# Spare products for PE in the idle gaps of a transformer block's head, and evacuations chosen by what is ready

## Chip, cores, metric

One core of a Trainium2 chip. The metric is device microseconds of one execution, median over the timed executions. PE is TensorE, ACT ScalarE, DVE VectorE, POOL GpSimd, SP the engine that issues most transfers.

## The reference

A pre-norm transformer block on 2048 tokens of width 1024: multi-query attention (32 query heads of 32, one key and value head), then a gated feed-forward part of width 3584, both with a residual. Cut to what matters:

```python
h  = x + A(layernorm(x), wq, wk, wv, wo)          # softmax((x@wq) @ (x@wk).T * Dh**-0.5) @ (x@wv) @ wo
h2 = h + B(layernorm(h), w_gate, w_up, w_down)    # (sigmoid(g) * u) @ w_down
```

## The kernel before

The kernel is written by a scheduler of its own: a Python plan with an estimated duration for each instruction decides, at build time, the order on every engine, and the program is then emitted in that order with semaphores. So an edit to the plan can move instructions far from the edited line.

The head of the program normalizes the 16 tiles of x on DVE, turns tiles 0 to 3 by transposes on PE and the others by DMA, and makes K, V and the first Q. The kernel lays out eight banks in PSUM for what PE writes: two (`F_ps`) for Q, K, V, transposes and everything else, six (`S_ps`) in three pairs for scores. What leaves a bank is copied by ACT or DVE; `evac` chooses by the work already queued on each:

```python
def evac(fn_act, fn_dve, n, deps, prio, dve_rate=0.96):
    now = pl.free["pe"]
    a = max(pl.free["act"], now) + sum(o.occ for o in pl.heap["act"]) + n / 1.2
    d = max(pl.free["dve"], now) + sum(o.occ for o in pl.heap["dve"]) + n / dve_rate
    ...                                   # the smaller sum takes the copy (after the first scores with an offset for ACT)
# transposes of x tile t, half hf, leave their bank always by ACT:
e = pl.op("act", fa, [last], prio=1, **t_act(512))
```

When the plan finds nothing for PE, it issues a product whose result nobody reads, if an F_ps bank is free, else it lets PE wait:

```python
if v == 0 and known([c_w], t):            # v: score blocks issued so far; warm-up products
    pl.op("pe", mm(S_ps[:, 5, 0:P], hact[:, 0:P], hact[:, 0:P], True, True), [c_w], ...)
...
spare = [b for b in range(2) if known(bank_rel[b], t) and ...]
if v and spare:
    ...                                   # a product into the free F_ps bank
pl.free["pe"] = t + 20.0                  # otherwise PE waits
```

The softmax here doesn't subtract the row's maximum and nothing guards it: scores larger than these inputs give would overflow.

## Time and profile before

| | before |
|---|---|
| median of 3 runs | 1081.42 us (1079.97 to 1081.45) |
| span of the profiled run | 1079.0 us |
| PE busy | 1069.8 us, idle 9.2 us |
| clock of PE over the span | 0.998 of full |
| half clock | 19.358 to 22.771 us |

The prediction below shows the page, windows of 5 us and timelines. One more view is of use for what comes: the same windows laid so that they begin and end where the half clock does. The columns are start:end, length, busy time of PE, PE's weight loads, DVE, ACT and POOL (in brackets the instructions), the granted clock, the DMA share and GB/s.

```profile
15.94:19.36 3.42, 1.57 (x19) 1.06 (x20) 3.32 (x8) 3.42 (x7) 0.00 (x0) 1.00 0.87 306
19.36:22.77 3.41, 3.41 (x30) 2.20 (x28) 2.90 (x9) 0.67 (x3) 0.94 (x2) 0.50 0.02 5
```

In the first stretch PE works less than half of the time (1.57 of 3.42 us) at full clock; in the next its clock is 0.50 throughout.

The changes of the clock lie whole steps of 3.4133 us apart (3.413 in what follows). In this trace's clock record it is full from 5.705 us for 13.653 us (4 steps), half for 3.413 us (1 step), and full again for 1058.132 us (310 steps). I call a step a window, and the one just before a half clock the window that decided. That it decides is my reading, not something that a trace records.

### The profile page before, as it was taken

The numbers are of one execution on the slowest core, as the hardware profiler recorded it, in microseconds if no ns is written. First come the engines' busy times: TensorE is split into PE (matmuls) and PEld (weight loads), VectorE is DVE, ScalarE is ACT, GpSimd is POOL, SyncE is SP. The second block draws the span as 40 slices with busy tenths as digits, with TensorE's granted clock in tenths as the row PEclk, the third lists the DMA queues.
The fourth block names the chain that finished last, engine by engine and source line by source line (L and its number), as shares of the span: only waits on it lengthen the run. The fifth ranks groups of instructions, "written<-read, shape, count | busy, mean of one in ns | idle before, by whom it ended". The sixth has DMA issues, their size and how long they took to land.

```text
span 1079.0 us, 31597 instructions
## 1 busy us (share of the span) xinstructions
PE 1069.8 (99%) x13080; PEld 490.4 (45%) x13080; DVE 902.3 (84%) x1735; ACT 1009.7 (94%) x1168; POOL 30.7 (3%) x58
## 2 busy tenths in 40 slices
PE   8999999999999999999999999999999999999999
PEld 7764444444444444444444444444444444444445
DVE  7889998898989879898888989898887988888721
ACT  6999999999999999999999999999999999999700
POOL 2100000000000000000000000000000000000000
PEclk9999999999999999999999999999999999999999
DMA  8898898939679795969879594965969489887994
GB/s 227 166 282 267 210 286 229 269 92 285 169 210 220 154 278 123 271 141 253 198 177 272 133 277 105 277 168 155 264 168 275 108 232 201 217 224 162 287 275 113
DMA packets 308623, 227.14 MB, mean 211 GB/s; under 512 B 119808, under 2 KB 299904, under 8 KB 308480
## 3 DMA queue, kind: packets, MB, share of 16 engines
q1 hardware_dynamic: 307296, 224.92, 82.2%
q8 instruction: 103, 1.69, 0.7%
q14 instruction: 40, 0.33, 0.2%
q10 hardware_dynamic: 1184, 0.20, 0.1%
HBM read 195.17 MB, written 7.86 MB: 188 GB/s over the span
## 4 chain that ended last, share of the span: by engine, by line
PE 88%; ACT 10%; issue 1%; DMA 1%; DVE 1%; SPq 0%
PE F_ps L414 69%; PE S_ps L414 18%; ACT Pr L706 9%; ACT tnh L1008 1%; DMA ring<-in_B_w_up_dram 0%; DMA ring<-in_A_x_dram 0%; DVE Rc L805 0%; ACT zone L289 0%; DVE Ts L740 0%; DVE st L345 0%; ACT QTb L289 0%; PE F_ps L443 0%; DVE st L347 0%; DVE ring L383 0%; PE S_ps L443 0%
## 5 line engine op out<-in xcount | busy, mean ns | idle before, releaser
L706 ACT ACTIVATE Pr<-S_ps 128x1024 bf16<-128x1024 f32 x1024 | 970.1, 1168 | 4.1 <-PE S_ps L414 3.5
L740 DVE TENSOR_TENSOR Ts<-Ts,Pr 128x1024 bf16<-128x1024 bf16 x736 | 481.0, 676 | 33.9 <-ACT Pr L706 31.7
L414 PE MATMUL F_ps<-ring,hnT 128*128 128x512 bf16 (+1 forms) x1957 | 417.0, 380 | 1.7 <-issue 0.7
L414 PEld LDWEIGHTS F_ps<-ring,hnT 128*128 128x128 bf16 (+1 forms) x1957 | 147.7, 97 | 187.8 <-issue 48.5
L414 PE MATMUL F_ps<-zone,hact 128*128 128x512 bf16 (+2 forms) x1164 | 209.4, 377 | 0.7 <-issue 0.7
L414 PE MATMUL S_ps<-QTb,kT 32*128 32x256 bf16 x4096 | 207.2, 273 | 0.1
L414 PEld LDWEIGHTS S_ps<-QTb,kT 32*128 32x128 bf16 x4096 | 63.6, 92 | 206.8 <-ACT Pr L706 152.9
L414 PE MATMUL F_ps<-Pr,Vb 128*32 128x256 bf16 x4064 | 134.2, 274 | 0.0
L414 PEld LDWEIGHTS F_ps<-zone,hact 128*128 128x128 bf16 (+1 forms) x1164 | 75.0, 97 | 83.5 <-issue 23.0
L414 PEld LDWEIGHTS F_ps<-Pr,Vb 128*32 128x32 bf16 x4064 | 96.8, 96 | 29.9 <-issue 16.7
L740 DVE TENSOR_TENSOR Ts<-Pr 128x1024 bf16<-128x1024 bf16 x128 | 86.5, 683 | 25.7 <-ACT Pr L706 25.3
L1012 DVE SCALAR_TENSOR_TENSOR hst<-tnh,F_ps 128x512 bf16<-128x512 f32 x107 | 73.2, 684 | 38.4 <-PE F_ps L414 36.8
L1008 ACT ACTIVATE tnh<-F_ps 128x512 f32<-128x512 f32 x105 | 78.5, 747 | 5.7 <-PE F_ps L414 5.7
L414 PE MATMUL F_ps<-zone 128*128 128x256 bf16 (+4 forms) x667 | 75.7, 276 | 0.5 <-ACT QTb L289 0.4
L414 PE MATMUL F_ps<-wo_sb,OT 128*128 128x512 bf16 (+1 forms) x294 | 60.9, 380 | 0.2 <-issue 0.2
L414 PEld LDWEIGHTS F_ps<-zone 128*128 128x128 bf16 (+1 forms) x667 | 44.0, 98 | 23.1 <-issue 7.4
L747 DVE TENSOR_TENSOR Ts<-Ts 128x1024 bf16<-128x1024 bf16 x64 | 43.9, 686 | 1.1
L357 POOL TENSOR_SCALAR zb<-mvb 128x1 bf16<-128x1 bf16 (+1 forms) x25 | 9.9, 396 | 994.5 <-DVE mvb L349 994.5
L1008 ACT ACTIVATE tnh<-S_ps 128x512 f32<-128x512 f32 x7 | 4.2, 597 | 35.3 <-PE S_ps L414 35.3
L290 DVE COPY Oc<-F_ps 128x256 f32<-128x256 f32 x60 | 25.3, 421 | 11.5 <-PE F_ps L414 10.7
L414 PEld LDWEIGHTS F_ps<-wo_sb,OT 128*128 128x128 bf16 (+1 forms) x294 | 20.9, 97 | 26.7 <-issue 7.4
L795 DVE TENSOR_TENSOR Oc<-F_ps,Oc 128x256 f32<-128x256 f32 x59 | 24.9, 422 | 7.4 <-PE F_ps L414 6.2
(81 smaller groups left out, 414.2 us busy)
## 6 DMA issues: line engine op xcount, KB each, us to landing
ring<-in_B_w_gate_dram SPq DMA_DIRECT2D x318, 256.0 KB, 4.7
ring<-in_B_w_up_dram SPq DMA_DIRECT2D x316, 256.0 KB, 4.6
zone<-in_B_w_down_dram SPq DMA_DIRECT2D x28, 256.0 KB, 3.6
h_sb<-in_A_x_dram SPq DMA_DIRECT2D x16, 256.0 KB, 4.5
out_dram<-h_sb SPq DMA_DIRECT2D x31, 128.0 KB, 3.1
ring<-in_A_x_dram SPq DMA_DIRECT2D x7, 512.0 KB, 5.1
QTb<-q_scratch SPq DMA_DIRECT2D x14, 256.0 KB, 5.4
Pr<-in_B_w_gate_dram SPq DMA_DIRECT2D x10, 256.0 KB, 4.2
```

Of the source, the lines that this page charges most:

```text
L290: lambda: DVE.tensor_copy(out=out_ap, in_=in_ap))
L357: f = pl.op("pool", lambda: POOL.tensor_scalar(out=zb[:, ph, sl].unsqueeze(2), in0=mvb[:, ph, sl, 1:2], scalar1=LN_EPS_BF16, scalar2=None, ...
L414: fn = lambda: PE.matmul(o, lhsT=l, rhs=r, start=start, stop=stop, **kw)
L706: exps[u] = pl.op("act", lambda slot=slot, pb=pb: ACT.activation(out=pslot(slot).rearrange("p (a b) -> p a b", a=2), in_=S_ps[:, pb:pb + 2 ...
L740: o = pl.op("dve", lambda T=T, a=a, b=b: DVE.tensor_tensor(out=T, in0=a, in1=b, op=ALU.add), deps, prio=4, **t_dve(1024, 1.92))
L747: merge_ev[G] = pl.op("dve", lambda T4=T4: DVE.tensor_tensor(out=T4[:, :, 0, :], in0=T4[:, :, 0, :], in1=T4[:, :, 1, :], op=ALU.add), [sum ...
L795: a = pl.op("dve", lambda: DVE.tensor_tensor(out=Oc[:, :], in0=O, in1=Ob, op=ALU.add), [last, oc_ev[G], o_ev.get(G - 1)], prio=0, **t_dve( ...
L1008: tanh_of[n] = pl.op("act", lambda: ACT.activation(out=tnh[:, :], in_=FB(b), func=ACTF.Tanh, scale=0.5), [last, tn_user.get(0)] + (tn_more ...
L1012: e = pl.op("dve", lambda: DVE.scalar_tensor_tensor(out=hst[:, n % NST, :], in0=tnh[:, :], scalar=1.0, in1=FB(b), op0=ALU.add, op1=ALU.mul ...
```

## The change

Its intent: PE should not go idle in the head, so that the work there (and the clock) goes on; ACT, which is full there, should give copies to DVE while DVE waits for x. The diff in full:

```diff
 def evac(fn_act, fn_dve, n, deps, prio, dve_rate=0.96):
     now = pl.free["pe"]
-    a = max(pl.free["act"], now) + sum(o.occ for o in pl.heap["act"]) + n / 1.2
-    d = max(pl.free["dve"], now) + sum(o.occ for o in pl.heap["dve"]) + n / dve_rate
+    ready = now + 300.0 if v < 2 else 1e9
+    a = max(pl.free["act"], now) + sum(o.occ for o in pl.heap["act"] if o.ready <= ready) + n / 1.2
+    d = max(pl.free["dve"], now) + sum(o.occ for o in pl.heap["dve"] if o.ready <= ready) + n / dve_rate
@@ transposes of x @@
-    e = pl.op("act", fa, [last], prio=1, **t_act(512))
+    e = evac(fa, fd, 512, [last], 1) if t > 1 else pl.op("act", fa, [last], prio=1, **t_act(512))
@@ nothing found for PE @@
+    if 0 < v < 16 and not spare and known([exps[2 * v - 1]], t):
+        k = 2 * ((2 * v - 1) % NB)
+        enter("full")
+        pl.op("pe", mm(S_ps[:, k, 0:P], ident[:, :], ident[:, :], True, True), [c_id, exps[2 * v - 1]], **t_mm(P)).tag = "dummy"
+        continue
```

## The prediction

> **What bounds the kernel now.** I read the page first (busy shares, the clock row, the chain of work that ended last), then windows of the head, then the timelines of PE, ACT and DVE there.
>
> ```profile
> PE 1069.8 (99%) x13080; PEld 490.4 (45%) x13080; DVE 902.3 (84%) x1735; ACT 1009.7 (94%) x1168; POOL 30.7 (3%) x58
> PE 88%; ACT 10%; issue 1%; DMA 1%; DVE 1%; SPq 0%
> ```
>
> PE is idle for 1079.0 - 1069.8 = 9.2 us of the whole span, and PE and ACT together are 98% of the chain. So nothing that fills idle time can be worth 2% (21.6 us); what can be won is a few microseconds, and they lie in the head. Windows of 5 us show where:
>
> ```profile
> core 0: us, PE busy (x) PEld busy (x) DVE busy (x) ACT busy (x) POOL busy (x), PEclk, DMA share, GB/s
> 10.00:15.00 5.00, 5.00 (x99) 4.19 (x97) 4.00 (x11) 3.76 (x9) 1.12 (x2) 1.00 1.08 361
> 15.00:20.00 5.00, 3.01 (x38) 2.15 (x35) 3.96 (x10) 4.52 (x9) 0.55 (x2) 0.94 0.74 247
> 20.00:25.00 5.00, 5.00 (x72) 3.47 (x70) 3.21 (x10) 2.74 (x6) 0.40 (x1) 0.72 0.38 75
> 25.00:30.00 5.00, 4.55 (x61) 3.21 (x59) 4.41 (x13) 5.00 (x9) 0.92 (x2) 1.00 0.81 167
> ```
>
> PE loses 2 us at 15 to 20 us; then the granted clock falls to 0.72 on average while ACT is nearly half idle. Quarter-microsecond windows put the half clock (0.50) from about 19.36 to 22.77 us, 3.41 us long. The timeline of PE shows what came before it (start, length, what):
>
> ```profile
> 15.40 0.40 PE L443 MATMUL F_ps<-ident,ring 128*128 128x128 bf16 x4
> 16.59 0.89 PE L443 MATMUL F_ps<-ident,ring 128*128 128x128 bf16 x8 [0.80 <-ACT QTb L289]
> 18.49 0.40 PE L443 MATMUL F_ps<-ident,ring 128*128 128x128 bf16 x4 [1.01 <-ACT zone L289]
> 18.98 3.07 PE L414 MATMUL F_ps<-zone 128*128 128x128 bf16 x23
> 21.98 0.61 PE L414 MATMUL S_ps<-QTb,kT 32*128 32x256 bf16 x8
> ```
>
> From 15.40 to 18.98 PE does nothing but 16 transposes of x tiles 2 and 3, and it waits for ACT to empty the two F_ps banks. What ACT does then:
>
> ```profile
> 14.95 0.39 ACT L289 ACTIVATE QTb<-F_ps 128x256 bf16<-128x256 f32 x1
> 15.21 1.04 ACT L706 ACTIVATE Pr<-S_ps 128x1024 bf16<-128x1024 f32 x1
> 16.12 0.42 ACT L289 ACTIVATE QTb<-F_ps 128x256 bf16<-128x256 f32 x1
> 16.38 0.65 ACT L289 ACTIVATE zone<-F_ps 128x512 bf16<-128x512 bf16 x1
> 16.86 1.08 ACT L706 ACTIVATE Pr<-S_ps 128x1024 bf16<-128x1024 f32 x1
> 17.76 1.76 ACT L289 ACTIVATE zone<-F_ps 128x512 bf16<-128x512 bf16 x3
> 22.64 1.02 ACT L706 ACTIVATE Pr<-S_ps 128x1024 bf16<-128x1024 f32 x1 [1.67 <-PE S_ps L414]
> ```
>
> ACT works without a gap from 13.13 to 19.5 us, so here ACT sets PE's pace; then it starves until the slow PE delivers the next scores at 22.64. DVE meanwhile stands:
>
> ```profile
> 13.47 0.88 DVE L394 TENSOR_SCALAR ring<-ring,rstd 128x1024 bf16<-128x1024 bf16 x2
> 16.04 0.69 DVE L345 BATCH_NORM_STATS2 st<-ring 128x6 f32<-128x512 bf16 x1 [1.69 <-DMA ring<-in_A_x_dram]
> 24.05 0.23 DVE L290 CAST Vb<-F_ps 128x64 bf16<-128x64 f32 x1 [1.79 <-ACT kT L289]
> ```
>
> [...] half clock lasted 3413 ns, and the last clock change before it, at 5.705 us, lies four such windows ahead (5.705 + 4 x 3.413 = 19.357). So the window that decided was 15.944 to 19.357. [...] that window held 12 transposes (12 x 0.056 = 0.67 us at their spacing) and 7 matmuls (0.39 us), together 31%, and lost the clock; the next emptiest at full clock were at 67% or more and kept it. [...]
>
> **The change, part by part.** The three edits look as if the scheduler might reshuffle everything, so I compared the order of instructions on each engine. It hardly moves: SP and POOL are identical, and after the first half dozen score blocks nothing differs anywhere.
>
> *Evacuations.* Two QTb copies go from ACT to DVE and one Vb copy from DVE to ACT. The new choice for x tiles 2 and 3 changes nothing: their four zone copies stay on ACT. The first QTb copy (12.33) lay before the wait for the first scores (13.13) and is worth nothing. The second (14.95) lies in the gapless ACT stretch: 15.21 - 14.95 = 0.26 us earlier for all that follows, so the next F_ps copies, PE's transposes and the Q products at 18.98 come at about 18.7. On DVE the first delays the norm of tiles 2 and 3: a copy of 0.4 us, less the 0.21 us that DVE waits there for POOL anyway, some 0.2 to 0.3 us; they are ready near 14.6 and are used at 15.2 or later. The second falls into the 1.69 us in which DVE waits for x. Both are free. The Vb copy costs ACT about 0.10 us: a QTb copy of 0.38 us takes 0.26 us of ACT's time, and a Vb copy lasts 0.16 us less (0.22).
>
> *Products.* Fourteen products with the identity are added: nine after the third set of transposes, five after the fourth. At 0.056 us apart that is 0.50 and 0.28 us. The nine wait for the exponential at 16.86 (done near 17.6 after the shift); then PE would have waited till about 18.1 for its bank anyway. The five end near 18.7, where Q can start. They cost at most 0.05 us.
>
> *Clock.* The window 15.944 to 19.357 would now hold 12 transposes (0.67), 14 products (0.78) and Q products from 18.7 on (0.66): 2.1 us or 62%, against 31%. If that keeps full clock, these go away: nine 128-column matmuls at 0.107 instead of 0.056 us, 0.46; seven 256-column ones at 0.213 instead of 0.109, 0.73; from the first score matmul to its exponential 0.66 instead of 0.45 (as at 12.68 to 13.13), 0.21; the change to score mode 0.04. Sum 1.44 us.
>
> *Does it reach the end?* ACT is gapless again from 22.64 to 27.25, then PE runs from 27.30 with almost no wait, the same order as before. If all engines come earlier by the same amount, the end does too. Not everything moves: the transposes by DMA of tiles 4 and 5 still go out at 21.77, the second near 23.1; with 3.6 us to landing they are there near 27. They are first used near 30.4 us by my count of matmuls, 28.8 after the shift, so 1.8 us of slack. The later tiles hang on DVE, which no longer stands 1.79 us before a Vb copy, so they come earlier as well.
>
> Sum: 0.26 + 1.44 - 0.10 - 0.05 = 1.55 us at 27 us, carried whole to the end. 1081.4 - 1.55 is 1079.9; I say **1079.8 us**.
>
> **The rivals.**
> *A, the clock still falls.* The products are few, and [...] no window at full clock between 31% and 67% tells me where the limit is. Then 0.1 to 0.2 us are left: 1081.2. I give it one in four.
> *B, the half clock was not in every run before.* [...] the three timed runs were 1081.45, 1081.42 and 1079.97: the odd one is 1.46 us faster, just my 1.44. If before often escaped, after gains only 0.1 us on those runs, but its own time is the same 1079.8. What speaks against an escape as the rule: two timed runs and the profiled one (1081.3) are slow. B alters the difference, not the prediction.
> *C, a wait takes the place.* PE comes 1.6 us early and meets data not yet there: the transposes by DMA, the weights, or ACT, which is 94% busy. For it: DVE is full from 30 to 45 us. Against it: the weight loads are released by exponentials, which move too, and the order is the same. It would give back part: 1080.5 to 1081.
> *D, more comes out.* DVE freed by 1.8 us could take away small waits for its copies at 28 to 50 us; PE's idle time there is only some tenths: 1079.3.
>
> **Range and chances.** Main case two in three at 1079.8 with about 0.7 us to either side for run to run spread; A and C pull up to 1081.3. So 1078.7 to 1081.4 eight times in ten. Faster by over 2% or slower by over 2% would take 21.6 us, more than twice all of PE's idle time, and nothing late in the order changed: 0.005 each, 0.99 within 2%.
>
> **What would show it.** Right: the clock at 1.00 through 15 to 25 us; the 23 matmuls after the last transposes in about 1.65 us instead of 3.07; the third pair of exponentials starting near 21.0 instead of 22.64; no DVE wait for kT near 22 us; the span shorter by about 1.5 us. The evacuations alone are seen in Q starting near 18.7. Wrong if the half clock is still there or moved to another window (A), if PE shows new waits after 28 us for DMA or ACT (C), or if the products delay the fourth set of transposes beyond 18.2.

Passages are cut where marked: what was said there about the cause of the half clock, about transposes and about the order in which ACT and DVE work, none of which a trace of this case had shown when it was written. That the full clock, and with it the 1.44 us, would follow from a fuller window was at that time my estimate, from one trace with one window at 31% that lost the clock and none at full clock below 67%.

## The result

| | before | after |
|---|---|---|
| first round, 4 runs each | 1081.41 us (1079.97 to 1081.45) | 1080.24 us (1079.78 to 1080.59) |
| profiled span | 1079.0 us | 1078.0 us |
| clock over the span | 0.998 | 1.000 in all four runs |

The ratio is 0.9992, with a 95% interval of 0.9975 to 1.001: the same within 2%. Ratios are the mean time of one kernel's fast runs over that of the other's of the same rounds, so not quite the ratio of the medians quoted here.

The page of the changed kernel:

```profile
PE 1043.5 (97%) x12925; PEld 489.3 (45%) x13094; DVE 903.2 (84%) x1736; ACT 1009.8 (94%) x1167; POOL 30.6 (3%) x58
PE 73%; ACT 19%; issue 4%; DVE 2%; DMA 1%; SPq 0%; DVEq 0%
```

PE's 97% is no loss: 13094 weight loads stand beside 12925 matmuls, so 169 records of matmuls are missing in this trace. Where they are missing PE seems to wait for "issue" (from 100 to 1000 us 19.5 us in 112 waits, against 1.6 us in 6 in the kernel before). I therefore compare starts, not PE's busy time.

The same windows of 5 us as in the prediction:

```profile
15.00:20.00 5.00, 3.70 (x59) 3.17 (x57) 3.54 (x8) 4.41 (x9) 0.21 (x1) 1.00 0.76 263
20.00:25.00 5.00, 4.24 (x82) 3.28 (x83) 5.00 (x15) 4.28 (x8) 1.63 (x4) 1.00 0.29 55
```

The clock is 1.00 in both; from 20 to 25 us ACT is busy for 4.28 instead of 2.74 us, because scores reach it earlier. The timeline of PE in that stretch:

```profile
15.39 0.39 PE L444 MATMUL F_ps<-ident,ring 128*128 128x128 bf16 x4
16.46 0.89 PE L444 MATMUL F_ps<-ident,ring 128*128 128x128 bf16 x8 [0.69 <-ACT QTb L290]
17.87 0.68 PE L415 MATMUL S_ps<-ident 128*128 128x128 bf16 x9 [0.52 <-ACT Pr L707]
18.38 0.39 PE L444 MATMUL F_ps<-ident,ring 128*128 128x128 bf16 x4
18.61 0.44 PE L415 MATMUL S_ps<-ident 128*128 128x128 bf16 x5
18.89 1.82 PE L415 MATMUL F_ps<-zone 128*128 128x128 bf16 x23
20.64 0.40 PE L415 MATMUL S_ps<-QTb,kT 32*128 32x256 bf16 x8
```

The 9 and 5 products fill the wait before and after the fourth set of transposes, and the 23 matmuls take 1.82 instead of 3.07 us. ACT and DVE:

```profile
16.00 0.40 ACT L290 ACTIVATE QTb<-F_ps 128x256 bf16<-128x256 f32 x1
17.65 1.75 ACT L290 ACTIVATE zone<-F_ps 128x512 bf16<-128x512 bf16 x3
21.09 1.02 ACT L707 ACTIVATE Pr<-S_ps 128x1024 bf16<-128x1024 f32 x1 [0.72 <-PE S_ps L415]
```

```profile
14.48 0.42 DVE L291 CAST QTb<-F_ps 128x256 bf16<-128x256 f32 x1
16.45 0.69 DVE L346 BATCH_NORM_STATS2 st<-ring 128x6 f32<-128x512 bf16 x1 [1.55 <-DMA ring<-in_A_x_dram]
```

The exponential that began at 22.64 now begins at 21.09; the second moved copy lies on DVE in its wait for x.

Since the order is the same, each of the 1024 exponentials can be set beside its twin. I call the difference of their starts the **lead**. It is -0.15 us at the first pair (this execution's x simply came 0.15 us later), 1.55 us at the third, 1.45 from the moved Vb copy on, and 1.44 us as far as 125 us. Then something takes a part back: at 141 us it is 1.01, from 185 us to the end 0.97 us. The timeline of PE names it:

```profile
139.15 0.59 PE L415 MATMUL F_ps<-ring,hnT 128*128 128x512 bf16 x2 [0.43 <-DMA ring<-in_B_w_up_dram]
151.79 0.61 PE L415 MATMUL F_ps<-ring,hnT 128*128 128x512 bf16 x2 [0.86 <-DMA ring<-in_B_w_up_dram]
```

PE waits twice for weights that it did not wait for before. So three questions were open: does the clock make the gain, and which part of the change keeps it; does the kernel before always lose the clock; and are the late weights the price of the lead or chance?

### The profile page after: what moved, and what is told of

It reads as the page before. It is cut to its first block, busy times and chain, and to the rows that moved or that the text cites. A ratio compares the mean times of both kernels' runs of the same rounds, so it can differ in the third digit from the quotient of the medians.

```text
span 1078.0 us, 31453 instructions
## 1 busy us (share of the span) xinstructions
PE 1043.5 (97%) x12925; PEld 489.3 (45%) x13094; DVE 903.2 (84%) x1736; ACT 1009.8 (94%) x1167; POOL 30.6 (3%) x58
## 4 chain that ended last, share of the span: by engine, by line
PE 73%; ACT 19%; issue 4%; DVE 2%; DMA 1%; SPq 0%; DVEq 0%
PE F_ps L415 57%; ACT Pr L707 18%; PE S_ps L415 16%; ACT tnh L1009 1%; DVE Ts L741 1%; DMA ring<-in_B_w_up_dram 1%; DVE Rc L806 0%; DMA ring<-in_A_x_dram 0%; DVE st L346 0%; DVE Oc L796 0%; DVE hact L291 0%; DVE st L348 0%; PE F_ps L444 0%; DVE Oc L291 0%; DVE Ts L748 0%
## 5 line engine op out<-in xcount | busy, mean ns | idle before, releaser
L415 PE MATMUL F_ps<-ring,hnT 128*128 128x512 bf16 (+1 forms) x1870 | 400.7, 380 | 13.1 <-issue 8.5
L415 PE MATMUL F_ps<-zone,hact 128*128 128x512 bf16 (+2 forms) x1106 | 197.5, 377 | 9.5 <-issue 9.0
L415 PE MATMUL F_ps<-zone 128*128 128x256 bf16 (+4 forms) x658 | 72.2, 272 | 2.3 <-issue 1.1
L415 PE MATMUL F_ps<-wo_sb,OT 128*128 128x512 bf16 (+1 forms) x283 | 58.4, 380 | 1.7 <-issue 1.6
```

The source lines that it names most:

```text
L415: fn = lambda: PE.matmul(o, lhsT=l, rhs=r, start=start, stop=stop, **kw)
```

## The experiments

Each kernel ran five times, with nine runs of the kernel before on the same chip in between (three such groups of four kernels). For every execution the granted clock is recorded: 1.000, or 0.998 where it had one window of half clock (3.413 us at 0.50 in a span of 1079.0 us, in the first trace). I write "kept" and "lost" for these. All results were correct. Groups of five are small, so single counts (three lost, two kept) are weak; what the account rests on is all runs together.

### Evacuations alone, products alone, thin products, and the change again

The first experiment leaves out the products. The order on all engines is then that of the changed kernel, less 14 matmuls.

```diff
-            if 0 < v < 16 and not spare and known([exps[2 * v - 1]], t):
-                ...                      # the products
```

> The evacuation part alone: the order of instructions is that of the changed kernel less its 14 products. Theory (the clock makes the gain): PE loses the clock for one window of 3.41 us in the head again[...]; such runs take 1081.2 to 1081.6 us, and the profile's third pair of exponentials starts near 22.4 us. Rival (the evacuations make the gain, the products only fill idle time): 1080.3 us, no half clock needed for it.

Measured: 1081.1 us median; three runs lost the clock (1081.7, 1081.1, 1081.4), two kept it (1079.74, 1079.77). In the trace, which lost it, the lead is 0.27 us after the fourth exponential (0.32 less the 0.05 that it already had at the first); the third pair begins at 22.34.

```profile
18.16 0.40 PE L444 MATMUL F_ps<-ident,ring 128*128 128x128 bf16 x4 [1.01 <-ACT zone L290]
18.65 3.10 PE L415 MATMUL F_ps<-zone 128*128 128x128 bf16 x23
```

The 23 matmuls take 3.10 us at half clock, as before. The evacuations give their 0.27 us and do not keep the clock.

The second adds only the products, and leaves every copy where it was; PE's order differs from before in these 14 alone.

```diff
+            if 0 < v < 16 and not spare and known([exps[2 * v - 1]], t):
+                ...                      # the products; evac() and mk_xT() as before
```

> The 14 products alone, every evacuation where the kernel before had it: the order differs from before in these 14 matmuls only. Theory: full clock through the head in every run (granted clock 1.000), third pair of exponentials near 21.3 us instead of 22.64, some 1080.2 us. Rival (evacuations make the gain): 1081.4 us as before, with or without the half clock.

Measured: 1081.36 us; three lost (1081.59, 1082.62, 1081.36), two kept (1080.15, 1079.77). Here my theory, as I had put it, fell: the products alone do not keep the clock either.

```profile
18.12 0.74 PE L414 MATMUL S_ps<-ident 128*128 128x128 bf16 x9 [0.52 <-ACT Pr L706]
18.66 0.63 PE L443 MATMUL F_ps<-ident,ring 128*128 128x128 bf16 x4
19.62 2.98 PE L414 MATMUL F_ps<-zone 128*128 128x128 bf16 x23
```

The nine products are there, from 18.12 on, and the fourth set of transposes runs at half clock, which begins at 18.60. The window that decided, 15.185 to 18.598, ended as the ninth product started: it held nearly all of the nine, but neither the fourth set nor the five products after it.

The third is the changed kernel unedited, for a second trace.

> The changed kernel once more, unedited, for a second trace and five more rounds beside the others on one chip. If the 0.5 us given back between 125 and 165 us comes from a stretch in which the weight transfers fill the DMA engines, PE waits for weights there again (two waits of about 0.4 and 0.9 us in the first trace) and the lead falls from 1.44 to about 1.0 us. If that was chance in one run, the lead stays 1.44 to the end and the time is 1079.8 us.

Measured: 1079.82 us (1079.74 to 1079.96), all five kept. The lead is 1.60 us at 27 us and still 1.57 at 900 us, and PE has no wait for weights. So the late weights of the first trace are not the regular price of the lead.

The fourth lets each product stream 16 columns instead of 128.

```diff
-mm(S_ps[:, k, 0:P], ident[:, :], ident[:, :], True, True)
+mm(S_ps[:, k, 0:16], ident[:, :], ident[:, 0:16], True, True)
```

> The changed kernel with each of its 14 products streaming 16 columns instead of 128: same count, same places, same waits, but about an eighth of the streaming (14 x 0.025 us at the spacing of small matmuls). Theory (what counts is how much PE streams in a window): the half clock comes back in runs whose window falls on the transposes, 1081.2 to 1081.6 us. Rival (the presence of products, or their waits, makes the gain; streaming doesn't matter): 1080.3 us at full clock.

Measured: 1081.28 us; four lost (1080.95, 1081.28, 1081.51, 1081.42), one kept (1079.70). Count, places and waits are those of the changed kernel, so here it is the streaming of the products that counts, not that they are there. (The 0.025 us of the expectation can be seen in the first trace of before: 32-column matmuls start so far apart from 22.78 us on. On this chip 10 of these 15 runs of incomplete kernels lost the clock, 4 of the 9 of before, and none of the 5 of the changed kernel.)

### The kernel before again, and transposes in place of the products

> The kernel before, unedited, for a second trace and more runs. Theory [...]: about half of the runs lose the clock (granted clock 0.998) and take 1.0 to 1.5 us longer than those that keep it; if the traced run kept it, its windows, counted from its first full clock, all hold over 42% of streaming; if it lost it, the lost one holds under 37%. Rival (the loss belongs to the kernel, not to the phase): all runs lose it, at 1081.4 us.

(The cut parenthesis is the theory that a run loses the clock when a window happens to fall on the stretch of transposes; in the first six traces the windows there began anywhere from 14.19 to 15.94 us.) Measured: 1080.0 us, **all five kept** (1079.83 to 1080.37); the nine interleaved runs of the same kernel on the same chip kept it six times and lost it three times (1081.42, 1081.8, 1081.43). Here is the timeline of the same program as before, in an execution that kept its clock:

```profile
18.98 1.83 PE L414 MATMUL F_ps<-zone 128*128 128x128 bf16 x23
20.75 0.40 PE L414 MATMUL S_ps<-QTb,kT 32*128 32x256 bf16 x8
```

Up to 18.98 it is the execution of the prediction to the hundredth; then 1.83 instead of 3.07 us. Its lead over the first trace is 1.44 us from the third pair to the end, which is the price of one lost window measured by itself. The rival "the loss belongs to the kernel" falls. Where it kept the clock, windows of 3.413 us counted from its first full clock (4.146 us) hold 80, 37.5 and 63% of streaming; I had expected over 42% for the emptiest.

Next, the 14 products become 14 transposes of the identity:

```diff
-mm(S_ps[:, k, 0:P], ident[:, :], ident[:, :], True, True)
+lambda k=k: PE.transpose(out=S_ps[:, k, :].bitcast(BF16)[:, 0:P], in_=ident[:, :], identity=ident[:, :])
```

> The changed kernel with its 14 products turned into 14 PE transposes of the identity into the same idle score banks: same count, size, places and waits. If a transpose counts [...] like any matmul, the emptiest window stays as full as in the changed kernel (42 to 45% streaming in two traces) and no run of five shows the half clock: 1079.8 to 1080.3 us. If transposes don't count, the window is as empty as with the evacuation part alone and about half the runs show the half clock (granted clock 0.998) at 1081.1 to 1081.7 us.

Measured: 1079.78 us (1079.71 to 1080.27), all five kept. That speaks for transposes counting as well. It does not prove it: on that chip three runs of 14 of the kernel before lost the clock, and in this trace no window fell on the stretch (they held 65 and 70%).

With streaming taken as the columns of each matmul or transpose at 2.4 per ns (128 more columns cost 0.109 - 0.056 = 0.053 us at full clock), overlaps counted once, the window that decided is:

| trace | window from, us | streaming | without transposes | clock |
|---|---|---|---|---|
| evacuations alone | 15.58 | 28.1% | 9.4% | lost |
| before, first | 15.94 | 29.1% | 10.4% | lost |
| thin products | 15.66 | 34.6% | 15.9% | lost |
| products alone | 15.18 | 36.8% | 18.0% | lost |
| before, again | 14.38 | 37.5% | 18.8% | kept |
| after, again | 14.19 | 42.3% | 23.6% | kept |
| after, first | 15.00 | 44.6% | 25.0% | kept |

Both columns order the traces without a fault, so the limit can be drawn as well with transposes (36.8 to 37.5%) as without (18.0 to 18.8%), and neither is shown. By the first, about half of all phases should lose the clock in the kernel before (on its first trace windows that begin from 14.4 to 16.2 us, 1.8 of 3.413); of its 32 runs in the three groups 10 did, so what exactly is counted stays open. If every phase of the window is tried on the changed kernel's trace, the emptiest holds 41%; on the products alone 33%, on the evacuations alone 23%, on the kernel before 20%. If the limit lies between 36.8 and 37.5%, as in the table, only the changed kernel of these four has no phase that loses: that is why both parts are needed here. The evacuations let the second score block and five Q products change places (22 and 10 instead of 27 and 5 matmuls around it) and everything after come 0.27 us sooner, which shortens the poor stretch on one side; the products shorten it on the other.

### More products, and where the instruction packets fall

If filling is good, filling earlier should do it alone. The score pair freed by the exponential before the last two is idle sooner; with it, 52 products fill all gaps between the four sets of transposes, without any moved copy. The same was tried on top of the changed kernel (47 products in the trace, 13127 matmuls; the expectation says 46).

```diff
-            if 0 < v < 16 and not spare and known([exps[2 * v - 1]], t):
-                k = 2 * ((2 * v - 1) % NB)
+            free = 2 * v - (3 if v == 2 else 1)
+            if 0 < v < 16 and not spare and known([exps[free]], t):
+                k = 2 * (free % NB)
```

> No evacuation is moved; the products go into the score pair that is free earlier (the exponential before the last two instead of the last), so 52 of them fill the gaps between all four sets of transposes. Theory (streaming in the emptiest window decides, and the evacuations only helped by bringing work into it): the clock is kept in every run without the evacuation part, 1079.9 to 1080.3 us; the run of 21 may delay the fourth set by 0.2 to 0.4 us. Rival (the evacuation part is needed for the clock): some runs at 0.998 and 1081.4 us.

> The changed kernel with its products in the score pair that is free earlier: 46 in the same stretch instead of 14. Theory: the clock is kept in every run as in the changed kernel already, so no more is to be had: 1079.8 us, or up to 0.3 us more if the run of 21 products ahead of the fourth set of transposes holds PE beyond the release of its bank. Rival (more products win more): below 1079.5 us.

Measured: all ten runs are recorded as kept, and tried at every phase the emptiest window holds 67 and 57%; that fits the theory that the gaps cost the clock. (The trace of the first kernel holds no clock record; its 23 matmuls take 1.82 us, as at full clock.) The run of 21 products did not delay the fourth set of transposes: 18.45 us against 18.49 before. Yet the times are 1081.67 us (1080.75 to 1082.5) and 1080.63 us (1079.75 to 1081.8), where unedited runs of before that kept the clock on that chip take 1079.72 to 1080.37. I had not foreseen this. In the head nothing is lost: the lead of the first of the two is 1.40 us at 27 us (1.49 less the 0.09 of its start). A wait of 0.6 us for weights near 141 us takes nothing that lasts, and the lead goes a thousand microseconds later:

```profile
1032.59 1.04 PE L414 MATMUL F_ps<-zone,hact 128*128 128x512 bf16 x4 [0.83 <-DMA hact<-hst]
```

PE waits 0.83 us for a DMA transpose of the feed-forward activations, and the lead falls from 1.49 to 0.49. The second kernel's trace does not have this wait; late weights at 133 and 142 us take its lead from 1.38 to 0.29, so that slow run is not explained by what follows. The DMA records show one 16 KB packet at 1029.6 us on the queue that the page calls "q8 instruction", beside the transposes that SP issued at 1027.3 and 1028.6; it took 0.96 us. In the changed kernel's second trace such packets lie at 1020.2 and 1036.7 instead. The changed kernel's first trace holds 103 of them, beside 13094 weight loads and as many matmuls of PE: 254 to a packet. (In the first trace of before, which lacks no record, 252 in the median start between one packet and the next.) So I estimate that these packets bring PE's instructions, some 250 each, and that 38 more pairs of weight load and matmul shift every later one by about 0.3 of their distance. No trace says which engine a packet is for. A new theory, then: the place of the packet costs the time, not the products. To test it, the products of the warm-up at the very start are cut in two, which adds instructions and leaves the rest of the order alone:

```diff
+                if n_split[0] < 38:      # 30 in the second kernel
+                    n_split[0] += 1
+                    for h in range(2):   # twice 64 columns instead of once 128
+                        pl.op("pe", mm(S_ps[:, 5, h * 64:h * 64 + 64], hact[:, 0:P], hact[:, h * 64:h * 64 + 64], True, True), [c_w], ...)
+                    continue
```

> The changed kernel with 38 of the 50 warm-up products at its very start cut into two of half the columns: the same streaming there, nothing else moved, but 38 more pairs of PE instructions, as many in all as the early-products kernel had (13132 matmuls). Theory (the slow times of the early-products kernels at full clock come from where the fetches of PE's instructions fall: the longer stream puts a 16 KB fetch beside the DMA transposes near 1029 us): full clock in every run, yet 1080.7 to 1082.5 us, with a PE wait of about 1 us for a DMA transpose near 1031 us. Rival (the early products themselves do it, or chance): 1079.7 to 1080.3 us, no such wait.

> The early-products kernel with 30 of its warm-up products cut in two: another 30 pairs of PE instructions[...]. Theory (place of the fetches): full clock in every run and the wait near 1031 us gone or elsewhere; 1079.9 to 1080.5 us. Rival (the early products cost it): 1080.7 to 1082.5 us as before.

> The early-products kernel unedited, beside the two with cut warm-up products on one chip. If its slow times are a property of the kernel: full clock, 1080.7 to 1082.5 us again, with the wait near 1031 us in the trace. If they were chance or the chip: 1079.8 to 1080.4 us.

> The changed kernel unedited as anchor for the others on this chip: full clock in all runs, 1079.7 to 1080.3 us, lead over the first trace of before 1.6 us from 25 us on, less 0.4 to 1.0 us where weights are late between 130 and 152 us, in some runs.

What the expectations call a fetch is such a packet. Measured on one chip, all runs kept:

| kernel | matmuls | median, us | runs | instruction packet near 1030 us |
|---|---|---|---|---|
| after, third | 13094 | 1079.76 | 1079.63 to 1080.01 | 1037.2 |
| after, warm-up cut (38) | 13132 | 1081.56 | 1081.21 to 1083.23 | 1032.3 |
| early products, again | 13132 | 1081.69 | 1080.33 to 1082.18 | 1029.1 |
| early products, warm-up cut (30) | 13162 | 1080.78 | 1080.19 to 1081.02 | 1024.9 |

The line of PE at that place, for the changed kernel with the cut warm-up, for the early products again, and for the early products with cut warm-up:

```profile
1035.05 1.04 PE L416 MATMUL F_ps<-zone,hact 128*128 128x512 bf16 x4 [0.99 <-DMA hact<-hst]
```

```profile
1033.87 1.04 PE L414 MATMUL F_ps<-zone,hact 128*128 128x512 bf16 x4 [0.94 <-DMA hact<-hst]
```

```profile
1026.57 6.47 PE L415 MATMUL F_ps<-zone,hact 128*128 128x512 bf16 x28
```

The same line in the third trace of the changed kernel:

```profile
1026.24 6.21 PE L415 MATMUL F_ps<-zone,hact 128*128 128x512 bf16 x28
```

38 pairs at the start, where nothing else changed, bring the wait at the same instruction: 28 matmuls without a break become 24, a wait, and 4. (Just before that wait the cut kernel's traced run is 2.5 us later than the third run of the changed one, 1.4 of it from a late load of wq at 12 us and 1.0 from late weights near 143 us in that run, so its packet at 1032.3 lies where 1029.8 would be.) In the traces the wait costs 1.0 to 1.2 us of lead; the rest of the 1.8 us in the median is not traced to it. And 30 more pairs under the early products leave 0.26 us of that wait (the 28 matmuls take 6.47 instead of 6.21 us), and take 0.9 us off the median. The packet moves roughly as counted: 38 matmuls of 512 columns at a spacing of 0.216 us are 8.2 us; measured from the first of the 28 matmuls, the packet comes 11.0 us later in the third trace of the changed kernel, 3.6 with the cut warm-up, 3.2 and 1.5 in the two traces of the early products. That the number of PE's instructions decides about this wait is shown by two kernels with the same number and different heads, and two with the same head and different numbers. That it works by the packet standing in the way of the transpose is argued from their places: in these three traces, and in none of the other eleven, a packet starts between the issue of the transpose and its use. No run forced it. The kernel with 30 cut products is also still 1.0 us slower than the changed one in the median, above the 1080.5 us that I had allowed; its smaller lead in the head (1.40 against 1.60 us) explains 0.2. Its trace, of its fastest run, keeps that lead as far as 1014 us, and the rest stays open.

The waits for weights near 130 to 152 us appear in seven traces (the first of the changed kernel, evacuations alone, early products with 0.6 us, after with early products, early products again, after with cut warm-up, and 0.2 us with transposes as products) and not in the others, with and without a lead; no run settles what delays those transfers in one execution and not in the next.

No kernel tried beats the changed one.

## Why the prediction was right

It predicted 1079.8 us; the first round measured 1080.24, two later rounds 1079.82 and 1079.76, all inside the range. By its steps:

- **Same within 2%**: right, since PE had only 9.2 us of idle time.
- **Order of instructions**: right; the first 25 us decide, the rest is the same order.
- **Evacuations, 0.26 us, less 0.10 for the Vb copy**: right; 0.27 us after the fourth exponential with the evacuations alone, and the lead falls by 0.10 at the Vb copy in every trace that has it.
- **Products cost at most 0.05 us**: right; Q starts at 18.89, 18.74 after taking off that run's late start of 0.15, where 18.7 was said. The fourth set of transposes, named as a sign, starts at 18.23 after the same correction (18.2 was the mark).
- **Clock, 1.44 us**: right to the hundredth; the kernel before with and without the loss differs by 1.44 us from the third pair of exponentials to the end. One sign was misreckoned: the 23 matmuls take 1.82 us, not 1.65, since the 1.65 is the sum of their spacings and the timeline runs to the end of the last; 3.07 was read from the timeline.
- **1.55 us at 27 us, carried whole to the end**: 1.60 us (1.45 + 0.15) in the first trace, 1.58 to 1.60 in the next two, and whole to the end in those two. In the first trace 0.5 us went to late weights, rival C by its look; but later runs show that it is not the lead that causes it.
- **The window "15.944 to 19.357"**: this is the step that failed. The prediction reckoned the new contents of one window at the place it had in one execution. The window lay elsewhere in every execution traced, and in the changed kernel's first two traces it began at 15.00 and 14.19 (in the third, none fell on the stretch). 62% was never measured there; 44.6 and 42.3% were, not far above the 37.5% that just kept the clock. It also gave the evacuations no part in the clock, and without them it is lost in three of five runs. That the margin was enough at every phase was luck as far as this reckoning goes.
- **Rival B**: it said that an escape of the kernel before was not the rule. It is the rule: of 32 runs of before in the three groups 22 kept the clock (mean 1080.12 us) and 10 lost it (mean 1081.44). So most runs had little to gain. On the two chips where both kernels ran side by side in these groups, before has a mean of 1080.72 us (18 runs; 1080.29 for the 11 that kept the clock) and the changed kernel 1079.82 (10 runs, all kept): 0.90 us, of which 0.43 is the lost clock, 0.17 the evacuations (0.27 - 0.10), and the rest is not explained. The intervals of the ratio there (0.9979 to 1.0004) still contain 1. What tells the kernels apart is the recorded clock: with the rate of before, 22 of 32, fourteen kept runs of fourteen would come by chance in about 0.5% of cases. The first 1.2 us came from a round in which three of the four runs of before took 1081.4 us.
- **That the products would keep the clock**: right for the change as a whole (14 of 14), wrong for the products alone (three of five lost).

## What to carry to other kernels

Where a short gap of PE leaves a window with little streaming, as here (lost at 28.1 to 36.8%, kept at 37.5 to 44.6%), the loss comes and goes with the place of the window, which was another in every trace of the table (15.94 and 14.38 us in two executions of one program): look at the recorded clock of every run before crediting an edit, and judge a stretch by its emptiest possible window, not by the one that a trace happens to show. Fill it at its ends or with work that must be done anyway, since here spare instructions were not free even where PE was idle: with 38 more pairs came a wait of 0.99 us a thousand microseconds on (1035.05 us), to judge by the places of the packets through a moved instruction packet. Compare starts of the same instruction in two traces of the same order; it shows where a gain arises and where it is given back far better than busy shares do.
